# Attention scores of every chunk as float32 products, instead of float32r parts in half of them

## The chip, the cores and the metric

The kernel runs on one core of a Trainium2 chip. The metric is the device time of one launch in microseconds (us), the median of three runs.

## The reference

The program is an attention layer followed by two feed-forward blocks, on two batches of 768 positions. Cut to what matters:

```python
scores = q @ k.T / sqrt(64) + bias          # 8 heads of 64, bias falls with the distance
scores = where(is_global | is_local, scores, -1e9)   # 8 global keys, 96 keys back
a = softmax(scores);  x = a @ v             # (2, 768, 512)
h = relu(x @ w_in)                          # 512 -> 1024
y = (h * sigmoid(conv3(h))) @ w_out         # 1024 -> 512, three taps along the sequence
h = relu(y @ w_in2);  u, v = halves of h
out = (u * (w_spatial @ layernorm(v) + b)) @ w_out2
```

All inputs are float32. q and k enter only in the scores.

## The kernel before

The sequence of each batch is cut into 3 chunks of 256 positions, which gives 6 groups (`g` from 0 to 5). In a group there are 4 units (`u`, a pair of heads each), and in a unit 2 steps (`s`, 128 queries each): 48 steps in all. For one step the following is queued, by the helpers named:

- `qk_load` brings q and k of a unit in one transfer of 336 KB into a tile `qk` (3 buffers). For groups that are not in `NATS` it also makes two parts of it: `qh`, the tile rounded to float32r (cast on ACT), and the rest `qk - qh`, again as float32r, written over `qk` (a subtraction on POOL or DVE, L492 through the helper `parts`).
- `scores` makes the products of both heads of the step on PE (L852). For a group in `NATS` it is one float32 product of `qk` with itself for each head, which the trace shows as two MATMUL records. For the others it is three float32r products for each head: part by part, without the product of the two rests.
- `soften` adds the bias and takes the largest score (L871, DVE), and from group 2 on adds a constant to it (`nb`, L884, POOL or DVE); then the exponential on ACT (L889). `halves` splits the result into float16 parts (`ph`), and a DMA transposes them. `weigh` multiplies with v (L957 for groups 0 and 1, L963 to L965 for the others) and divides by the sum on DVE (L969 to L974, result `xk`). `turn_x` transposes `xk` on PE (L1005) and makes the float16 parts of x.

Beside this run the two feed-forward stages of the first block: `inner` (L1081, 12 products for each of 8 slices of a group; the three taps on DVE, L1094; tanh on ACT; the gate on DVE, L1119) and `outer` (L1151). Their weights come as 64-bit floats and are decoded on ACT (L667) and DVE (L674, L677, L682, tile `wk`): 8 blocks each of the first block's two weights, then 4 blocks of `w3v` and 4 of `w3u` for the second block. After that PE alone carries the second block (L1226, L1299, L1331, L1361).

The order on each engine is written by a planner (`Plan`, lines 97 to 328). It takes every piece of work with a cost that is written beside it, simulates the engines for several rounds, chooses for pieces that two engines can do (POOL or DVE for a subtraction, ACT or DVE for a cast) the one that is done first in its model, and emits the instructions in that order; each engine then works strictly in order. It also puts throwaway matmuls (`warm`, L1052) where its model sees PE idle in the first 70 us. So a changed cost or a missing piece changes the order of the rest too. The cost that `scores` states for a step is 0.79 for float32 and 0.57 for the three float32r products:

```python
        if u // NPAIR in NATS:
            pairs = [(self.m("qk", u), self.m("qk", u))]
            cost, reads = 0.79, [("qk", u)]
        else:
            hi, lo = self.m("qh", u, dt=F32R), self.m("qk", u, dt=F32R)
            pairs = [(hi, hi), (lo, hi), (hi, lo)]
            cost, reads = 0.57, [("qk", u), ("qh", u)]
```

A second way through the program (`dense`) follows for counts beyond the reach of the banded way. It is behind a branch, does not run with these inputs, and the change leaves it alone.

Of the kernel before, what the change touches and what calls it, by code (L numbers as in the profile page):

```python
# [40 lines left out]

LEAD_TICKS, LEAD_STEPS = 12, 8

NATS, PLAINS = (0, 1, 2), (0, 1)

BIASES = 2

# [1589 lines left out]
```

## Time and profile before

| | us |
|---|---|
| runs | 386.78, 386.24, 386.82; median 386.78 |
| the profiled execution | 385.59 |
| its span, first to last instruction | 383.7 |
| outside the span | 1.9 |
| PE busy | 358.4 (93%) |
| DVE busy | 277.9 (72%) |
| ACT busy | 268.4 (70%) |
| POOL busy | 154.7 (40%) |

The durations below are of the one profiled execution, which lies 1.2 us under the median of the runs. All windows and times of the trace are counted from the start of the span. PE is TensorE, DVE VectorE, ACT ScalarE, POOL GpSimd.

### The profile page before, as it was taken

The page shows a single profiled execution, that of the slowest core. Times are in us where ns is not written, and L with a number is a line of the kernel's source. Part 1 is how long each engine was busy: PE and PEld are TensorE (multiplying, and loading weights), DVE is VectorE, ACT ScalarE, POOL GpSimd, SP SyncE. Part 2 cuts the span into 40 slices and gives each one's busy share as a digit, 9 for nine tenths or more (in the row PEclk, how much of TensorE's full clock was granted, in tenths as well). Part 3 has the DMA queues.
Part 4 walks back from the last instruction along what each step waited for, and adds up shares of the span by engine and source line. Part 5 has one row for each costly group of instructions (what it writes and reads, how often), then busy time and mean ns, then how long its engine had stood idle before and what let it go on. Part 6 is the DMA issues. An engine that isn't in the chain of part 4 may idle for free.

```text
span 383.7 us, 7835 instructions
## 1 busy us (share of the span) xinstructions
PE 358.4 (93%) x2852; PEld 252.6 (66%) x2852; DVE 277.9 (72%) x715; ACT 268.4 (70%) x659; POOL 154.7 (40%) x225
## 2 busy tenths in 40 slices
PE   8998788789899999989899999999999999999992
PEld 5777575557778888868689766765456665555541
DVE  5799999998997899999996399881667354241501
ACT  4989797788967999898795499789947434242420
POOL 5254426895778587569653054030205100000000
PEclk9999999899999999999899999999999999999998
DMA  7979523293849557883657000450200000102021
GB/s 221 407 238 296 186 68 91 49 217 109 186 99 240 150 135 128 223 200 57 97 116 297 2 2 0 126 164 2 94 1 2 0 2 15 68 3 81 2 109 64
DMA packets 46254, 43.60 MB, mean 114 GB/s; under 512 B 34816, under 2 KB 36608, under 8 KB 45696
## 3 DMA queue, kind: packets, MB, share of 16 engines
q1 hardware_dynamic: 46208, 43.03, 40.7%
q8 instruction: 24, 0.39, 0.4%
q14 instruction: 22, 0.18, 0.1%
HBM read 31.48 MB, written 3.15 MB: 90 GB/s over the span
## 4 chain that ended last, share of the span: by engine, by line
PE 61%; DVE 21%; ACT 6%; issue 5%; DMA 3%; POOL 2%; SPq 0%; DVEq 0%; POOLq 0%
PE bank L1331 12%; PE bank L1151 10%; PE bank L1081 9%; PE bank L1299 8%; PE bank L1361 8%; PE bank L1226 8%; DVE bank L1094 4%; DVE wk_dt_float L677 3%; DVE sb_dt_float L871 3%; DVE wk_dt_float L682 2%; PE bank L852 2%; DVE wk_dt_float L674 2%; DVE ac_dt_float L1119 2%; ACT sb_dt_float L889 1%; DMA raw_dt_float<-in_w3v 1%
## 5 line engine op out<-in xcount | busy, mean ns | idle before, releaser
L1081 PE MATMUL bank<-x_dt_float,w1h_dt_float 128*128 128x260 f16 (+1 forms) x384 | 65.5, 273 | 5.7 <-DVE xk_dt_float L974 2.5
L1151 PE MATMUL bank<-hh_dt_float,w2l_dt_float 128*128 128x254 f16 (+2 forms) x192 | 53.6, 279 | 1.1 <-POOL w2l_dt_float L492 1.1
L1151 PE MATMUL bank<-hh_dt_float,w2h_dt_float 128*128 128x254 f16 (+2 forms) x192 | 53.8, 280 | 0.2 <-DVE ac_dt_float L1119 0.2
L1151 PE MATMUL bank<-hl_dt_float,w2h_dt_float 128*128 128x254 f16 (+2 forms) x192 | 53.5, 279 | 0.0
L1081 PE MATMUL bank<-x_dt_float,w1l_dt_float 128*128 128x260 f16 (+1 forms) x192 | 52.4, 273 | 0.0
L1094 DVE SCALAR_TENSOR_TENSOR bank<-hp_dt_float,cwt,bank 128x254 f32<-128x254 f32 (+2 forms) x96 | 46.2, 486 | 6.4 <-ACT bank L1088 3.6
L1331 PE MATMUL bank<-ws_dt_float,vn_dt_float 128*128 128x384 f16 x288 | 47.3, 326 | 0.0
L1081 PEld LDWEIGHTS <-w1h_dt_float 128*128 128x128 f16 x384 | 36.6, 97 | 13.2 <-issue 7.6
L492 POOL TENSOR_TENSOR hl_dt_float<-ac_dt_float,hh_dt_float 128x254 f16<-128x254 f32 (+2 forms) x47 | 33.8, 727 | 24.3 <-ACT hh_dt_float L478 21.0
L492 POOL TENSOR_TENSOR ph_dt_float<-sb_dt_float,ph_dt_float 128x512 f16<-128x512 f32 x30 | 38.4, 1283 | 11.6 <-ACT ph_dt_float L478 8.5
L1151 PEld LDWEIGHTS <-w2h_dt_float 128*128 128x128 f16 x384 | 37.0, 100 | 7.3 <-issue 0.7
L1331 PEld LDWEIGHTS <-vn_dt_float 128*128 128x128 f16 x288 | 28.2, 98 | 18.8
L871 DVE CUSTOM_DVE_ANT_0 sb_dt_float<-bank,bias_dt_float 128x256 f32<-128x256 f32 (+1 forms) x96 | 35.0, 401 | 4.7 <-POOL qk_dt_float32r L492 1.7
L889 ACT ACTIVATE sb_dt_float<-sb_dt_float,nb_dt_float 128x256 f32<-128x256 f32 (+1 forms) x64 | 29.6, 493 | 10.5 <-POOL nb_dt_float L884 9.1
L478 ACT CAST g_dt_float<-bank 128x384 f16<-128x384 f32 x16 | 7.7, 479 | 33.8 <-DVE bank L1338 33.8
L1299 PE MATMUL bank<-ys_dt_float,w3uh_dt_float 128*128 128x384 f16 x128 | 31.2, 326 | 0.0
L1335 DVE SCALAR_TENSOR_TENSOR bank<-bank,bb_dt_float 128x384 f32<-128x384 f32 x16 | 9.1, 567 | 29.1 <-PE bank L1331 29.1
L1361 PE MATMUL bank<-w4h_dt_float,g_dt_float 128*128 128x512 f16 (+1 forms) x104 | 28.8, 363 | 0.0
L1226 PE MATMUL bank<-w3vh_dt_float,ys_dt_float 128*128 128x512 f16 x96 | 28.6, 379 | 0.0
L1361 PEld LDWEIGHTS <-g_dt_float 128*128 128x128 f16 x156 | 15.2, 98 | 15.8
L677 DVE SCALAR_TENSOR_TENSOR wk_dt_float<-raw_dt_float,wk_dt_float 128x512 int32<-128x512 int32 x28 | 24.9, 898 | 0.1
L1226 PEld LDWEIGHTS <-ys_dt_float 128*128 128x128 f16 x144 | 14.1, 98 | 15.6
(172 smaller groups left out, 894.0 us busy)
## 6 DMA issues: line engine op xcount, KB each, us to landing
raw_dt_float<-in_w SPq DMA_DIRECT2D x20, 512.0 KB, 5.4
qk_dt_float<-in_qk SPq DMA_DIRECT2D x24, 336.0 KB, 3.9
v_dt_float<-in_vb SPq DMA_DIRECT2D x4, 1024.0 KB, 5.7
out_x<-wk_dt_float SPq DMA_DIRECT2D x11, 256.0 KB, 2.0
raw_dt_float<-in_wst SPq DMA_DIRECT2D x6, 384.0 KB, 4.4
raw_dt_float<-in_w3v SPq DMA_DIRECT2D x4, 512.0 KB, 5.2
raw_dt_float<-in_w3u SPq DMA_DIRECT2D x4, 512.0 KB, 6.3
v_dt_float<-in_vb SPq DMA_DIRECT2D x2, 768.0 KB, 5.9
```

The costliest lines, as they stand in the source:

```text
L492: self.engines[e].tensor_tensor(out=out, in0=in0, in1=in1, op=ALU.subtract)
L677: nc.vector.scalar_tensor_tensor(out=fi, in0=lo, scalar=29, in1=fi, op0=ALU.logical_shift_right, op1=ALU.bitwise_or)
L871: nc.vector.tensor_tensor_reduce(out=sb[:, h, :n], in0=self.ps(self.sp[s][h])[:, :n], in1=self.m("bias", 2 * p + h)[:, t0 : t0 + n], scale ...
L889: nc.scalar.activation(out=sb[:, h, :n], in_=sb[:, h, :n], func=AF.Exp, scale=-1.0, bias=nb[:, h : h + 1])
L1081: nc.tensor.matmul(self.ps(acc)[:, :nx], w[f][:, k * P : (k + 1) * P], x[:, k, x0:], start=k == n == 0, stop=k == 3 and n == 2,)
L1094: nc.vector.scalar_tensor_tensor(out=ac(), in0=near(j), scalar=tap(j), in1=ac(), op0=ALU.mult, op1=ALU.add)
L1151: nc.tensor.matmul(ps(), w[2 * d + k // 4][:, k % 4 * P : (k % 4 + 1) * P], x, start=k == n == 0, stop=k == 7 and n == 2,)
L1226: nc.tensor.matmul(ps(), x[:, y, k, tk], w[k], start=n == 0, stop=n == 11)
L1299: nc.tensor.matmul(ps(), w[e4][:, k * P : (k + 1) * P], x[:, y, k, s], start=n == 0, stop=n == 11)
L1331: nc.tensor.matmul(ps(), v[:, k, x, ek], w[:, k, s], start=n == 0, stop=n == 17)
L1335: nc.vector.scalar_tensor_tensor(out=ps(), in0=ps(), scalar=2.0 ** -(self.k["v"] + self.k["s"]), in1=bb, op0=ALU.mult, op1=ALU.add)
L1361: nc.tensor.matmul(ps(), x[:, y, k, tk], w[k][:, at], start=n == 0, stop=n == 11)
```

## The change

Groups 3, 4 and 5 join groups 0, 1 and 2 in `NATS`. Their 12 units are then not split: 12 casts to `qh` and 12 subtractions go, and the 24 steps of these groups make two float32 products instead of six float32r products. The planner gets neither the split nor the lower cost for these steps and writes a new order for everything.

```diff
-NATS, PLAINS = (0, 1, 2), (0, 1)
+NATS, PLAINS = (0, 1, 2, 3, 4, 5), (0, 1)
```

What the planner makes of it is shown at two places, both on DVE. The first is at the start of group 3's `inner` slices (the tiles `hp` and `ac` belong to them), some 160 us into the program. Before, a decode of `w3v` (L674, L677, tile `wk`) lies between the taps, ahead of the division that gives `xk`:

```order
L1094 SCALAR_TENSOR_TENSOR bank<-hp_dt_float_180,cwt,bank 128x254 x2
L1119 SCALAR_TENSOR_TENSOR ac_dt_float_177<-bank,hp_dt_float_176 128x254
L674 TENSOR_SCALAR wk_dt_float_125<-wk_dt_float_125 128x512
L1119 SCALAR_TENSOR_TENSOR ac_dt_float_181<-bank,hp_dt_float_180 128x254
L677 SCALAR_TENSOR_TENSOR wk_dt_float_125<-raw_dt_float_140,wk_dt_float_125 128x512
L1094 SCALAR_TENSOR_TENSOR bank<-hp_dt_float_184,cwt,bank 128x254 x2
L969 TENSOR_SCALAR r_dt_float_158<-bank,cs_dt_float_215 128x4
L973 RECIPROCAL r_dt_float_158<-r_dt_float_158 128x4
L974 TENSOR_TENSOR xk_dt_float_150<-bank,r_dt_float_158 128x256
```

After the change, from the row behind the first one above, the same stretch of DVE reads:

```order
L1119 SCALAR_TENSOR_TENSOR ac_dt_float_177<-bank,hp_dt_float_176 128x254
L492 TENSOR_TENSOR x_dt_float_154<-bank,x_dt_float_153 128x256
L1119 SCALAR_TENSOR_TENSOR ac_dt_float_181<-bank,hp_dt_float_180 128x254
L1094 SCALAR_TENSOR_TENSOR bank<-hp_dt_float_184,cwt,bank 128x254 x2
L871 ISA sb_dt_float_137,nm_dt_float_151<-bank,bias_dt_float_307 128x256
L871 ISA nm_dt_float_151 128x1
L871 ISA sb_dt_float_137,nm_dt_float_151<-bank,bias_dt_float_313 128x256
L871 ISA nm_dt_float_151 128x1
L1119 SCALAR_TENSOR_TENSOR ac_dt_float_185<-bank,hp_dt_float_184 128x254
L969 TENSOR_SCALAR r_dt_float_158<-bank,cs_dt_float_210 128x4
L973 RECIPROCAL r_dt_float_158<-r_dt_float_158 128x4
L974 TENSOR_TENSOR xk_dt_float_150<-bank,r_dt_float_158 128x256
```

The decode of the `w3v` blocks has left the stretch; it follows when the slices of this group are done.

The second place is late in the lead, where the last blocks of `w2` are decoded while group 1's attention runs, some 66 us into the program. The rows marked - are of before, those marked + of the change:

```order
 L682 SCALAR_TENSOR_TENSOR wk_dt_float_125<-raw_dt_float_124,wk_dt_float_125 128x512
+L674 TENSOR_SCALAR wk_dt_float_127<-wk_dt_float_127 128x512
+L674 TENSOR_SCALAR wk_dt_float_134<-wk_dt_float_134 128x512
+L677 SCALAR_TENSOR_TENSOR wk_dt_float_127<-raw_dt_float_126,wk_dt_float_127 128x512
+L677 SCALAR_TENSOR_TENSOR wk_dt_float_134<-raw_dt_float_133,wk_dt_float_134 128x512
 L969 TENSOR_SCALAR r_dt_float_158<-bank 128x4
 L973 RECIPROCAL r_dt_float_158<-r_dt_float_158 128x4
 L974 TENSOR_TENSOR xk_dt_float_150<-bank,r_dt_float_158 128x256
-L674 TENSOR_SCALAR wk_dt_float_127<-wk_dt_float_127 128x512
-L674 TENSOR_SCALAR wk_dt_float_134<-wk_dt_float_134 128x512
```

Here four instructions of the decode moved ahead of the division that PE's L1005 waits for.

## Rows read from the trace of the kernel before

**Rows 1.** The page: its span, and the chain that ended last by engine.

```profile
span 383.7 us, 7835 instructions
...
PE 61%; DVE 21%; ACT 6%; issue 5%; DMA 3%; POOL 2%; SPq 0%; DVEq 0%; POOLq 0%
```

**Rows 2.** Windows: length, busy us of PE, PEld, DVE, ACT, POOL, then PE's granted clock, DMA.

```profile
70.00:75.00 5.00, 4.87 (x27) 3.34 (x28) 5.00 (x12) 3.17 (x10) 3.54 (x4) 0.66 0.12 13
...
110.00:155.00 45.00, 45.00 (x478) 36.28 (x476) 39.40 (x122) 39.45 (x92) 31.84 (x50) 1.00 0.70 160
155.00:185.00 30.00, 26.86 (x311) 22.23 (x308) 28.35 (x80) 25.45 (x67) 22.18 (x31) 1.00 0.66 152
180.00:185.00 5.00, 3.66 (x51) 3.06 (x49) 4.93 (x13) 2.61 (x6) 3.62 (x6) 1.00 0.32 61
185.00:190.00 5.00, 4.53 (x26) 3.37 (x26) 5.00 (x10) 3.78 (x11) 4.70 (x4) 0.66 0.39 74
...
200.00:375.00 175.00, 175.00 (x1116) 107.23 (x1114) 94.68 (x179) 99.21 (x241) 27.96 (x36) 1.00 0.16 55
```

**Rows 3.** Waits of PE from 76 to 204 us: total, times, longest.

```profile
PE bank L1005 <- DVE xk_dt_float L974: 2.7, 3, 1.8
PE bank L1081 <- DVE xk_dt_float L974: 1.2, 1, 1.2
PE bank L963 <- DVE ac_dt_float L1119: 1.2, 2, 0.8
PE bank L776 <- DVE vm_dt_float L757: 1.0, 1, 1.0
```

**Rows 4.** The same view from 0 to 76 us.

```profile
PE bank L1005 <- DVE xk_dt_float L974: 3.1, 2, 2.4
```

**Rows 5.** PE's timeline, a float32 and a float32r step: start, duration, instruction.

```profile
79.42 0.70 PE L852 MATMUL bank<-qk_dt_float 64*128 64x256 f32 x4
80.06 0.28 PE L1151 MATMUL bank<-hh_dt_float,w2h_dt_float 128*128 128x254 f16 x1
...
87.62 0.39 PE L852 MATMUL bank<-qh_dt_float32r 64*128 64x256 f32 x2
...
88.17 0.28 PE L1151 MATMUL bank<-hh_dt_float,w2h_dt_float 128*128 128x254 f16 x1
```

**Rows 6.** Lines by form: the split of q and k, and a DVE subtraction.

```profile
L492 POOL TENSOR_TENSOR qk_dt_float32r<-qk_dt_float,qh_dt_float32r 128x672 fp32r<-128x672 f32 x10 | 16.6, 1661 | 3.8 <-ACT qh_dt_float32r L478 2.0 <-DMA qk_dt_float<-in_qk 1.6
...
L478 ACT CAST qh_dt_float32r<-qk_dt_float 128x672 fp32r<-128x672 f32 x12 | 8.9, 744 | 0.8 <-DMA qk_dt_float<-in_qk 0.8
...
L492 DVE TENSOR_TENSOR qk_dt_float32r<-qk_dt_float,qh_dt_float32r 128x672 fp32r<-128x672 f32 x2 | 2.7, 1328 | 0.0
L492 DVE TENSOR_TENSOR ph_dt_float<-sb_dt_float,ph_dt_float 128x512 f16<-128x512 f32 x2 | 2.6, 1303 | 0.0
```

**Rows 7.** DVE's timeline at group 3's slices: the `w3v` decode among them.

```profile
161.87 1.17 DVE L674 TENSOR_SCALAR wk_dt_float<-wk_dt_float 128x512 int32<-128x512 int32 x1
...
163.29 1.06 DVE L677 SCALAR_TENSOR_TENSOR wk_dt_float<-raw_dt_float,wk_dt_float 128x512 int32<-128x512 int32 x1
```

**Rows 8.** DVE's timeline before the stop at 183.7 us.

```profile
179.64 1.11 DVE L884 TENSOR_TENSOR nb_dt_float<-nm_dt_float,shift 128x2 f32<-128x2 f32 x1
...
182.57 0.41 DVE L488 SCALAR_TENSOR_TENSOR ys_dt_float<-bank,ys_dt_float 128x258 f16<-128x258 f32 x1
...
184.20 0.42 DVE L674 TENSOR_SCALAR wk_dt_float<-wk_dt_float 128x512 int32<-128x512 int32 x1
```

**Rows 9.** DVE's timeline behind the division at 68.1 us.

```profile
68.43 1.93 DVE L674 TENSOR_SCALAR wk_dt_float<-wk_dt_float 128x512 int32<-128x512 int32 x2
70.28 1.64 DVE L677 SCALAR_TENSOR_TENSOR wk_dt_float<-raw_dt_float,wk_dt_float 128x512 int32<-128x512 int32 x1
...
72.53 0.95 DVE L677 SCALAR_TENSOR_TENSOR wk_dt_float<-raw_dt_float,wk_dt_float 128x512 int32<-128x512 int32 x1
```

**Rows 10.** DVE's timeline early: the wait before the first division.

```profile
14.15 0.16 DVE L969 TENSOR_SCALAR r_dt_float<-bank 128x4 f32<-128x4 f32 x1 [1.61 <-PE bank L957]
```

## The prediction

> **What bounds the kernel now.** I read the page's span and chain first, then windows by stage, then PE's waits, then the timelines at the waits. The chain names PE for 61% and DVE for 21% of the span [rows 1], so the question is where which of the two leads. The windows answer it: from 110 to 155 us PE is busy for all of its 45 us, and from 200 to 375 us for all of its 175 us [rows 2]. There only PE's own work counts, and nothing that DVE, ACT or POOL are spared brings anything. From 155 to 185 us it is the other way: PE is busy for 26.9 of 30 us, DVE for 28.4 [rows 2]. The waits say for what PE stands still there: the longest are 1.8 us and 1.2 us for `xk`, the division on DVE [rows 3]. The lead, up to 85 us, is of the same kind, with a wait of 2.4 us for `xk` as its longest [rows 4]. Twice the granted clock of TensorE falls from 2.4 to 1.2 GHz: in the windows 70 to 75 and 185 to 190 us its mean is 0.66 [rows 2], which is 3.4 us at half speed and so about 1.7 us of work lost each time. Both falls come after PE stood still: after the wait of 2.4 us, and after 180 to 185 us, where PE is busy for 3.7 of 5 us [rows 2, 4].
>
> So the program's time is PE's work, plus PE's waits before 200 us, plus the two slow stretches, plus the end. The change touches the first three.
>
> **The change part by part.**
>
> *The products themselves (PE, slower).* A float32 step with float16 neighbours goes from 79.42 to 80.06 us until the next matmul starts, 0.64 us; a float32r step from 87.62 to 88.17 us, 0.55 us [rows 5]. The other steps repeat this pattern to 0.01 us. The difference, 0.09 us less rounding, is 0.08 us. With 24 steps that is +2.0 us, on the engine that sets the end. This price needs no bound, since both forms are in the trace. By the Trainium skill, "FP8 and Floating Point Precision", section "TensorE Precision Notes", a true float32 product takes four passes through the array. Read with one pass for each float32r product that makes four in place of three, +0.18 us for a step, 4.4 us in all and a sum that is 2.4 us worse; the rows speak against it here, since the four records of the float32 step take 15% longer than the six of the other, not 33%.
>
> *The split (ACT, POOL, DVE: removed).* 12 casts of 0.74 us on ACT, 10 subtractions of 1.66 us on POOL, 2 of 1.33 us on DVE [rows 6]: 8.9, 16.6 and 2.7 us of busy time. ACT and POOL end no long wait of PE after 76 us [rows 3], so what they are spared counts at zero by itself, covered by DVE's queue; if DVE were not the late one, POOL would be. The 2.7 us on DVE are real only where DVE leads, and the planner gives part of them away: it now puts one subtraction of a `w2` block on DVE in the lead, and one of `ph` there too. The nearest row is the `ph` subtraction, of the same size, 1.30 us [rows 6]: +2.6 us against one split subtraction of 1.3 us gone from that stretch. Against that it moves the first decode into a wait of 1.6 us which DVE has at 14 us [rows 10], of which I count all. The lead then comes to 2.6 - 1.3 - 1.6 = -0.3 us. The ends are +1.3 us (nothing of that wait is used) and -1.6 us (the added subtractions find room); I take **-0.5 us**, the middle less a little for POOL's emptier queue.
>
> *The decode of `w3v` among group 3's slices (DVE, moved).* Two decode instructions of 1.17 and 1.06 us stand between the taps just before the division that PE waits 1.2 us for [rows 3, 7]. In the new order they follow after the slices. So this wait should go. They are not gone from DVE, though: they still run before the next long wait, the one of 1.8 us at 183.7 us. Ahead of that one three others leave: the addition of `nb` (1.11 us, now on POOL), an instruction of `ys` (0.41 us) and one L674 (0.42 us), both put behind the division [rows 8]. Start to start, less 0.08 us of overlap each for the last two, that is 1.8 us which DVE is early. PE however comes earlier too: by the 1.2 us of the wait that went, less 5 steps of 0.08 us that lie between the two places, so by 0.8 us. The wait at 183.7 us then is 1.8 - 1.8 + 0.8 = 0.8 us. Both together fall from 3.0 us to 0.8 us, **-2.2 us**. Bounds: 0, if the first wait only moves to the second place; -3.0 us, if both go.
>
> *The slow stretch at 185 us.* With a wait of 0.8 us in place of 1.8 us, and none some us before, I expect the clock to stay at 2.4 GHz: **-1.7 us**. Bounds: 0 and -1.7.
>
> *Waits added.* None by the change itself: the scores now wait for the load of `qk` alone, where they waited for a cast and a subtraction behind it. The throwaway matmuls go from 42 to 38; they lie in PE's idle time, so they count at zero unless the clock falls in their place.
>
> *Sum.* +2.0 - 0.5 - 2.2 - 1.7 = -2.4 us. The profiled execution took 385.6 us (383.7 us of span and 1.9 us around it), which gives 383.2 us; it lies 1.2 us under the median of the runs, so against the median of 386.8 us the forecast is **384.4 us**.
>
> **The rivals.** What a measurement can tell from no change is about 0.2%, 0.8 us; that is the border between the cases.
>
> *The clock falls all the same at 185 us.* PE is busy for only 3.7 of 5 us there [rows 2], and part of that idle time may be spread over small waits. Then the sum is -0.7 us: 386.1 us, just inside the border.
>
> *The waits only move (slower).* DVE is busy for 28.4 of the 30 us from 155 us [rows 2]. If the decode, now in one lump after the slices, holds up the division at 183.7 us by what the earlier place gained, neither wait nor slow stretch goes: +2.0 - 0.5 = +1.5 us, 388.3 us. It decides from the point at which that wait is 3 us or more. For it: the lump stands on DVE right ahead of that place; against it: three instructions left the same queue [rows 8].
>
> *The lead stops longer (slower).* At the wait of 2.4 us in the lead [rows 4] four decode instructions now stand ahead of the division instead of behind it. Behind it they take 1.93, 1.64 and 0.95 us [rows 9], 4.3 us start to start. If the wait grows by that, if it isn't given back by a shorter queue afterwards, and if the slow stretch that follows lasts twice as long (1.7 us), the sum is +2.0 + 4.3 + 1.7 - 2.2 - 1.7 = +4.1 us: 390.9 us. For it: DVE is busy for all of the 5 us from 70 us [rows 2], so it is what counts there. Against it: the same work is no longer behind the division, so DVE should be early for what comes next; the lead's end is then the same.
>
> *A larger relief.* POOL's queue shrinks by a tenth, and DVE's L674 takes 1.17 us in one place and 0.42 us in another [rows 7, 8], on the same shape. If the longer times come from POOL's subtractions running beside it, less POOL work shortens DVE's too. Then both waits go (-3.0), and those of 1.2 and 1.0 us from 85 us on [rows 3] with them: +2.0 - 0.5 - 3.0 - 1.7 - 2.2 = -5.4 us, 381.4 us. Taking the lead at its bound of -1.6 us it is 380.3 us. By the Trainium skill, "SBUF — State Buffer", section "Who interferes with whom", DVE and GpSimd share one pair of ports, which one of them holds for a whole instruction, so that the other blocks. The two durations agree with it; the sum with it is this rival's, and it has no share in the forecast's.
>
> *Four passes,* as weighed above: 386.8 us, no change.
>
> *The split isn't gone.* It is: in the new order no float32r instruction is left in the part that runs.
>
> **How the numbers follow.** The forecast 0.46; the clock falls all the same 0.15; the waits only move 0.11; the lead stops longer 0.11; the larger relief 0.13; four passes 0.04. Faster by over 0.2% are the forecast, the larger relief and somewhat under half of the clock's case: 0.65. Within 0.2% are the rest of that case, four passes, and a small part of the waits that only move: 0.15. Slower is what is left: 0.20. The likeliest case alone, with its bounds for the lead and for the second wait, goes from 382.6 to 386.2 us. The range for 8 in 10 leaves out the lead that stops longer and the last part of the larger relief, and takes in the waits that only move: 380.8 to 388.4 us.
>
> **What would show it.** Right: L852 has 192 float32 records, and a step takes 0.64 us; no L492 and L478 with float32r tiles; PE's wait for `xk` around 164 us is gone and the one near 183 us under 1 us; the granted clock is at 2.4 GHz from 180 to 200 us; from 110 us to about 155 us and from 200 us PE is still busy without a gap. Wrong: a second slow stretch that stays, PE's waits after 150 us still 3 us in sum, or waits in the lead, 0 to 76 us, that grow by more than 2 us. If steps took 0.74 us, the price of the products would be the failed step.

## The result, and the profile after

The kernel after takes **383.26 us** (median of 5 runs, 382.01 to 384.14), the kernel before 386.78 us: a ratio of 0.991, with a 95% interval from 0.9885 to 0.9935. That is 3.5 us, or 0.9%, faster. The profiled execution took 382.87 us and has a span of 381.0 us, against 385.59 and 383.7 us.

First the page of the kernel after: the span, the busy time of each engine, the chain by engine.

```profile
span 381.0 us, 7688 instructions
...
PE 358.0 (94%) x2800; PEld 248.5 (65%) x2800; DVE 270.4 (71%) x710; ACT 260.5 (68%) x646; POOL 137.2 (36%) x219
...
PE 59%; DVE 15%; ACT 10%; POOL 7%; issue 6%; DMA 2%; POOLq 0%; DVEq 0%; ACTq 0%
```

PE is busy for as long as before (358.0 and 358.4 us), although its products became dearer; one slow stretch of its clock fewer (below) is part of the reason. DVE lost 7.5 us of busy time, ACT 7.9 and POOL 17.5. In the chain DVE fell from 21 to 15% [rows 1], ACT rose from 6 to 10% and POOL from 2 to 7%.

The step is the first term of the prediction. The timeline of PE (start, duration, instruction), a float32 step of group 3 and what follows it:

```profile
114.80 0.70 PE L852 MATMUL bank<-qk_dt_float 64*128 64x256 f32 x4
115.43 0.44 PE L1005 MATMUL bank<-ident,xk_dt_float 128*128 128x128 f32 x2
```

From one start to the next it is 0.63 us. The 24 steps of groups 3 to 5 now all look like this, where the float32r form took 0.55 us [rows 5].

The windows of the kernel after, with the columns of [rows 2]:

```profile
70.00:75.00 5.00, 4.65 (x41) 3.80 (x38) 5.00 (x14) 3.38 (x10) 3.50 (x4) 1.00 0.96 101
110.00:155.00 45.00, 44.25 (x457) 34.02 (x455) 37.62 (x118) 35.73 (x85) 22.68 (x44) 1.00 0.64 148
155.00:185.00 30.00, 29.27 (x295) 22.76 (x293) 27.43 (x74) 26.50 (x71) 20.86 (x31) 1.00 0.64 160
180.00:185.00 5.00, 4.32 (x33) 3.12 (x32) 4.97 (x7) 2.75 (x7) 5.00 (x5) 1.00 0.56 107
185.00:190.00 5.00, 4.22 (x51) 3.30 (x51) 4.19 (x17) 2.49 (x6) 3.47 (x4) 1.00 0.56 105
200.00:375.00 175.00, 173.32 (x1091) 105.07 (x1087) 94.00 (x179) 95.62 (x232) 30.54 (x37) 1.00 0.16 55
```

From 155 to 185 us PE is busy for 2.4 us more than before. Both windows with a clock of 0.66 are now at 1.00, which is 2.4 GHz. One slow stretch, 3.4 us at half speed, stands early, where the kernel before had none:

```profile
25.00:30.00 5.00, 4.38 (x22) 2.75 (x22) 4.86 (x18) 4.30 (x12) 2.46 (x3) 0.71 0.60 161
```

PE's waits from 76 to 204 us, which answer to [rows 3], in total, times, longest:

```profile
PE bank L1005 <- DVE xk_dt_float L974: 1.3, 2, 0.6
PE bank L963 <- DVE ac_dt_float L1119: 1.3, 2, 0.8
PE bank L852 <- DVE nm_dt_float L871: 0.8, 1, 0.8
```

and from 0 to 76 us [rows 4]:

```profile
PE bank L1005 <- DVE xk_dt_float L974: 3.4, 2, 2.8
PE bank L1081 <- DVE nm_dt_float L871: 2.1, 1, 2.1
```

The wait of 1.2 us for `xk` in front of L1081 is gone, and the one of 1.8 us. In their place stand shorter ones, and a new one of 2.1 us in the lead.

The two kernels can be set against each other at one place in any order of the rest: the transpose of the last division (L1005), after which PE works alone. Of before, and below it of after:

```profile
206.57 0.38 PE L1005 MATMUL bank<-ident,xk_dt_float 128*128 128x128 f32 x2
```

```profile
203.71 0.38 PE L1005 MATMUL bank<-ident,xk_dt_float 128*128 128x128 f32 x2
```

It comes 2.86 us earlier. Behind it 177.1 and 177.3 us are left, the same. So in these two executions, whose spans differ by 2.7 us, the whole gain arose before 206 us. The question of the experiments is by which of the change's three parts: dearer products, no split, another order.

### The profile page after: what moved, and what is told of

Read it like the earlier page. It is cut to its first block, busy times and chain, and to the rows that moved or that the text cites. A ratio compares the mean times of both kernels' runs of the same rounds, so it can differ in the third digit from the quotient of the medians.

```text
span 381.0 us, 7688 instructions
## 1 busy us (share of the span) xinstructions
PE 358.0 (94%) x2800; PEld 248.5 (65%) x2800; DVE 270.4 (71%) x710; ACT 260.5 (68%) x646; POOL 137.2 (36%) x219
## 4 chain that ended last, share of the span: by engine, by line
PE 59%; DVE 15%; ACT 10%; POOL 7%; issue 6%; DMA 2%; POOLq 0%; DVEq 0%; ACTq 0%
PE bank L1331 12%; PE bank L1151 8%; PE bank L1299 8%; PE bank L1361 8%; PE bank L1226 8%; PE bank L1081 6%; PE bank L852 3%; DVE bank L1094 3%; DVE sb_dt_float L871 3%; ACT sb_dt_float L889 3%; DVE wk_dt_float L677 2%; POOL ph_dt_float L492 2%; DVE wk_dt_float L682 2%; POOL hl_dt_float L492 2%; ACT ph_dt_float L478 2%
## 5 line engine op out<-in xcount | busy, mean ns | idle before, releaser
L1081 PE MATMUL bank<-x_dt_float,w1h_dt_float 128*128 128x260 f16 (+1 forms) x384 | 65.3, 273 | 3.0 <-DVE nm_dt_float L871 2.1
L1151 PE MATMUL bank<-hh_dt_float,w2h_dt_float 128*128 128x254 f16 (+2 forms) x192 | 52.4, 273 | 1.0 <-DVE nm_dt_float L871 1.0
L1151 PE MATMUL bank<-hl_dt_float,w2h_dt_float 128*128 128x254 f16 (+2 forms) x192 | 52.3, 272 | 0.5 <-POOL hp_dt_float L1103 0.4
L1081 PE MATMUL bank<-x_dt_float,w1l_dt_float 128*128 128x260 f16 (+1 forms) x192 | 52.3, 273 | 0.0
L1151 PE MATMUL bank<-hh_dt_float,w2l_dt_float 128*128 128x254 f16 (+2 forms) x192 | 52.3, 272 | 0.0
L492 POOL TENSOR_TENSOR ph_dt_float<-sb_dt_float,ph_dt_float 128x512 f16<-128x512 f32 x30 | 37.3, 1249 | 22.7 <-ACT ph_dt_float L478 19.3
L1081 PEld LDWEIGHTS <-w1h_dt_float 128*128 128x128 f16 x384 | 36.7, 97 | 9.9 <-issue 4.6
L889 ACT ACTIVATE sb_dt_float<-sb_dt_float,nb_dt_float 128x256 f32<-128x256 f32 (+1 forms) x64 | 29.5, 492 | 15.3 <-POOL nb_dt_float L884 14.5
L852 PE MATMUL bank<-qk_dt_float 64*128 64x256 f32 x192 | 34.6, 441 | 0.8 <-DVE nm_dt_float L871 0.8
L677 DVE SCALAR_TENSOR_TENSOR wk_dt_float<-raw_dt_float,wk_dt_float 128x512 int32<-128x512 int32 x28 | 27.4, 982 | 0.2
```

The lines of the kernel that those rows point to most:

```text
L492: self.engines[e].tensor_tensor(out=out, in0=in0, in1=in1, op=ALU.subtract)
L677: nc.vector.scalar_tensor_tensor(out=fi, in0=lo, scalar=29, in1=fi, op0=ALU.logical_shift_right, op1=ALU.bitwise_or)
L852: nc.tensor.matmul(self.ps(sp[h])[:, :256], x[r, t * P : (t + 1) * P], y[r, k0 : k0 + 256], start=n == 0, stop=n == len(pairs) - 1,)
L889: nc.scalar.activation(out=sb[:, h, :n], in_=sb[:, h, :n], func=AF.Exp, scale=-1.0, bias=nb[:, h : h + 1])
L1081: nc.tensor.matmul(self.ps(acc)[:, :nx], w[f][:, k * P : (k + 1) * P], x[:, k, x0:], start=k == n == 0, stop=k == 3 and n == 2,)
L1151: nc.tensor.matmul(ps(), w[2 * d + k // 4][:, k % 4 * P : (k % 4 + 1) * P], x, start=k == n == 0, stop=k == 7 and n == 2,)
```

## The experiments

Theories at the start. **A**, the prediction's: the products cost 2.0 us, the split is worth little by itself, the new order takes PE's waits away. **B**: the removed work itself is the gain. **C**: only slow stretches of the clock count. Each experiment was run 6 to 12 times beside runs of the kernel before on the same chip (median there 386.35, 386.66 and 387.00 us in the three groups of four). The ratios and their 95% intervals are to those; they go by the single runs and so differ by up to 0.4% from the quotients of the medians. A difference between two experiments is taken from their ratios; from the intervals I estimate that it is uncertain by about 0.3%, 1.2 us.

**The three parts, one at a time.** The planner is left in the belief that the work is as before, so the order stays that of before, word for word; only the emitted instructions change.

The first kernel has the products of after and no split:

```diff
-            pairs = [(hi, hi), (lo, hi), (hi, lo)]
+            pairs = [(self.m("qk", u), self.m("qk", u))]
...
-        self.parts(
-            CH + KW, self.m("qh", u, dt=F32R), self.m("qk", u, dt=F32R), self.m("qk", u),
-            [("qk", u)], [("qh", u)], [("qk", u)],
-        )
+        self.plan.add(copy_cost(CH + KW), lambda e: None, reads=[("qk", u)], writes=[("qh", u)])
+        self.plan.add(sub_cost(CH + KW), lambda e: None, reads=[("qk", u), ("qh", u)], writes=[("qk", u)])
```

> The order of before, with the 24 steps of groups 3 to 5 as float32 products and no instruction for the split (12 casts on ACT, 10 subtractions on POOL, 2 on DVE are gone; the planner still thinks they are there, so nothing else moves). Theory A (mine: the products cost +2.0 us, the split is worth little by itself, the new order takes PE's waits for xk away): +2.0 us, less up to 1.3 us for the DVE subtraction in the lead: 387.5 to 388.8 us against 386.8, PE's waits for xk at about 164 and 184 us still there, in sum 2 us or more. Theory B (the removed work itself is the gain: POOL's and DVE's relief shortens what PE waits for): 384 to 385.5 us in the old order too, with both waits gone. Theory C (only the granted clock counts, one slow stretch fewer): 388.8 us with a slow stretch near 70 and near 186 us, about 387 us with one of them gone, and no other difference.

Measured: 384.97 us, ratio 0.9951 (0.9928 to 0.9974), so 1.9 us faster than before. A, which expected it slower, falls. It is the time that B gave, but not B's way there: in this trace the first of PE's two waits for `xk` is as long as before, 1.24 us, and only the other shrank, from 1.81 to 1.13 us. And it is short of the kernel after.

The second makes the split, writes its rest over `qh` in place of `qk`, and reads neither:

```diff
-            CH + KW, self.m("qh", u, dt=F32R), self.m("qk", u, dt=F32R), self.m("qk", u),
+            CH + KW, self.m("qh", u, dt=F32R), self.m("qh", u, dt=F32R), self.m("qk", u),
```

> As the run before, but the 12 casts and 12 subtractions run as in the kernel before; what they write (the rounded copy, with the rest written over it) is read by nothing, and the products read q and k as loaded. This is the price of the products by itself. Theory A: 24 x 0.08 = +2.0 us, 388.8 us, within 0.5 us of it; the difference to the run without the split is what the removed work is worth, 0 to 1.3 us. Theory B: 388.8 us as well, but 3 us or more above the run without the split. Theory C: as A, where the slow stretches stay where they were.

Measured: 387.21 us, ratio 1.0011 (0.9988 to 1.0034). The products by themselves cost +0.4 us, with 2.0 us outside the interval (-0.5 to +1.3). The step itself has the price that the prediction gave it, so a part of it is covered, about half by the two profiled executions: PE is 1.60 us later than before at 162 us, 1.25 us later behind the two waits for `xk`, and 1.09 us at 207 us. (The products here no longer wait for the split either. That brought nothing where it could be seen: the one long wait of DVE that named POOL's split subtraction before, 1.67 us at 118.6 us, is 1.81 us here and names PE.) And the split that nobody reads is worth 0.6% of the time, 2.3 us, in an order that doesn't change.

The first kernel was run again, since its profiled execution had been its longest of 12:

> The kernel of the first experiment once more, unchanged, since its profiled execution was the longest of its 12 and its granted clock low for 6.8 us near 25 us and 13.6 us near 69 us. The worth of the split rests on it: 385.0 us again within 0.5 us, and in a profile with short slow stretches the tail behind the last division is 177.1 us and the last division comes at about 206 us, 1.7 us earlier than with the idle split.

Measured: 384.80 us, ratio 0.9943 (0.9918 to 0.9968), 2.6 us under the idle split. C falls as well: this execution has a slow stretch near 70 us and none at 186, for which C gave about 387 us, and took 385.01; and the mean clock of the 12 runs is 0.983, of the kernel before beside them 0.982. This trace has the order of before, so it can be laid over it row by row. PE's timeline from 182 us, of before:

```profile
185.47 0.44 PE L1005 MATMUL bank<-ident,xk_dt_float 128*128 128x128 f32 x2 [1.81 <-DVE xk_dt_float L974]
190.10 0.39 PE L852 MATMUL bank<-qh_dt_float32r 64*128 64x256 f32 x2
...
194.07 0.38 PE L1005 MATMUL bank<-ident,xk_dt_float 128*128 128x128 f32 x2
200.34 0.38 PE L1005 MATMUL bank<-ident,xk_dt_float 128*128 128x128 f32 x2
```

and of the old order without the split (the line that was shown, 206.57 us, is at 205.91 here), with the earlier wait of 1.2 us [rows 3] as its first row:

```profile
166.12 0.38 PE L1081 MATMUL bank<-x_dt_float,w1h_dt_float 128*128 128x256 f16 x2 [0.39 <-DVE xk_dt_float L974]
...
184.98 0.44 PE L1005 MATMUL bank<-ident,xk_dt_float 128*128 128x128 f32 x2 [1.12 <-DVE xk_dt_float L974]
187.95 0.70 PE L852 MATMUL bank<-qk_dt_float 64*128 64x256 f32 x4
192.31 0.44 PE L1005 MATMUL bank<-ident,xk_dt_float 128*128 128x128 f32 x2 [0.15 <-DVE xk_dt_float L974]
198.88 0.44 PE L1005 MATMUL bank<-ident,xk_dt_float 128*128 128x128 f32 x2
205.91 0.38 PE L1005 MATMUL bank<-ident,xk_dt_float 128*128 128x128 f32 x2
```

The slow stretch at 186 us is gone here too, in the old order. Follow the lead over before from 184.98 us on: 0.49 us there, 2.15 at the next row, then 1.76, 1.46 and 0.66 at the last. The full clock brings 1.7 us within 3 us of time, and 1.5 us of it is given back within the next 18, where waits for DVE and POOL appear that the slow PE had not had. DVE's own pace shows why: from the division that ends the second long wait to the last division it takes 20.02 us before, with the slow stretch, and 20.02 and 20.01 us in the idle split and here, without. **This slow stretch, in which PE was not the late engine, cost next to nothing.** Nor did a shorter wait prevent it: in the idle split's trace the wait ahead of it is still 1.60 us long, and the clock stays at 2.4 GHz.

In the lead it looks alike. In this trace the clock is low for 10 us from 71 us on:

```profile
70.00:75.00 5.00, 4.49 (x23) 3.30 (x23) 5.00 (x10) 2.83 (x10) 3.91 (x4) 0.63 0.16 21
75.00:80.00 5.00, 5.00 (x25) 4.05 (x25) 4.48 (x12) 4.12 (x9) 4.44 (x4) 0.50 1.10 194
80.00:85.00 5.00, 5.00 (x35) 3.06 (x34) 2.62 (x12) 2.71 (x9) 3.44 (x7) 0.85 0.88 262
```

and a transpose that stands at 78.41 us in before comes at 81.67, but one at 100.16 us comes at 100.44:

```profile
81.67 0.44 PE L1005 MATMUL bank<-ident,xk_dt_float 128*128 128x128 f32 x2
100.44 0.38 PE L1005 MATMUL bank<-ident,xk_dt_float 128*128 128x128 f32 x2
```

3.3 us behind, and 20 us later 0.3. But the split is missing between the two as well, and slow stretches are not free in general. The first run of this same kernel has 13.6 us at half speed there, and 6.8 us more near 25 us: it is 1.13 us later than this one at 75 us, still 1.13 us at 162 us, and 2.4 us from 168 us to the end, as its wait near 166 us is longer too. And of the 29 runs of the kernel before in the first group the nine with a mean clock up to 0.977 took 387.3 us in the median, the 13 with 0.986 or more 386.0 us. Their mean clocks differ by 0.016, which is 6.0 us of PE's work, and their times by 1.3 us: by this estimate some fifth of what a slower clock takes away reaches the end.

Against the idle split the trace of the second run is 1.75 us ahead at 207 us: 0.26 us of that at 111 us, 0.99 us at the wait near 166 us and 0.49 us at the one near 185 us. The next experiments show what acts at these two.

**What of the split counts.** First the two of its subtractions that stood on DVE, then the ten on POOL, are left out of the idle split, each by the engine that the planner chose:

```diff
-        self.parts(
...
+        qh, qk, drop = self.m("qh", u, dt=F32R), self.m("qk", u), ("DVE",)
+        self.plan.add(
+            copy_cost(CH + KW), lambda e: e in drop or self.copy(e, qh, qk), reads=[("qk", u)], writes=[("qh", u)],
+        )
+        self.plan.add(
+            sub_cost(CH + KW), lambda e: e in drop or self.minus(e, qh, qk, qh), reads=[("qk", u), ("qh", u)],
+            writes=[("qk", u)],
+        )
```

New theories: **D**, DVE's queue leads, and what DVE is spared counts; **E**, POOL's subtractions lengthen DVE's instructions beside them.

> The order of before, float32 products, the split run and read by nothing, but without the two of its subtractions that stood on DVE (2.7 us of busy time); the 12 casts on ACT and the 10 subtractions on POOL run. With the split whole the time was 387.2 us, without any of it 385.0. Theory D (new: before 206 us the queue of DVE leads and PE's extra 2.0 us are mostly covered, so what counts is what DVE is spared): 385 to 385.7 us. Theory E (what counts is POOL: its subtractions lengthen DVE's instructions that run beside them): 387.2 us within 0.6 us. Theory A: 386 to 387 us, the subtraction of the lead alone.

Measured: 386.93 us, ratio 1.0013 (0.9988 to 1.0038), as with the split whole. D falls in this form: 2.7 us less on the engine with the latest queue bring nothing that can be measured.

> The complement: the order of before, float32 products, the 12 casts on ACT and the two subtractions on DVE run and are read by nothing; the 10 subtractions on POOL (16.6 us) are gone. Theory D: 386.5 to 387.5 us, as with the split whole. Theory E: 385 to 385.7 us, as without it, and DVE's mean time of one instruction L674 or L677 lower than in the run with the split whole.

Measured: 386.45 us, ratio 0.9988 (0.9967 to 1.0009), 0.9 us under the idle split: a part, not the whole of E's 2 us, and less than the uncertainty. E's second sign is there in L674 (564 ns against 844 in the idle split, from 76 to 207 us), not in L677 (973 against 975).

Then the casts alone and all the subtractions alone. Theory **D2** is that the parts add up, **E2** that the subtractions hurt only together.

```diff
+        self.plan.add(copy_cost(CH + KW), lambda e: None, reads=[("qk", u)], writes=[("qh", u)])
+        self.plan.add(sub_cost(CH + KW), lambda e: self.minus(e, qh, qk, qk), reads=[("qk", u), ("qh", u)], writes=[("qk", u)])
```

> The order of before, float32 products, the 12 casts on ACT left out; the 12 subtractions run (qk less qk, read by nothing). Whole idle split 387.2 us, without DVE's share 386.9, without POOL's 386.5, without any 385.0: if the parts add up, the casts are worth the remaining 1.3 us, and this run gives 385.9 us, within 0.5 us (theory D2: ACT's queue ends waits too). If the subtractions only hurt together (POOL's and DVE's both in the way, theory E2), 387 us.

Measured: 385.36 us, ratio 0.9967 (0.9947 to 0.9988). Without the 12 casts on ACT the time falls by 1.7 us, though the subtractions all run. They no longer wait for a cast, as POOL's did in the idle split for 2.2 us, so this is not ACT's time alone.

```diff
+        self.plan.add(copy_cost(CH + KW), lambda e: self.copy(e, qh, qk), reads=[("qk", u)], writes=[("qh", u)])
+        self.plan.add(sub_cost(CH + KW), lambda e: None, reads=[("qk", u), ("qh", u)], writes=[("qk", u)])
```

> The order of before, float32 products, all 12 subtractions left out, the 12 casts run and are read by nothing. Theory D2: the casts' 1.3 us remain, 386.3 us. Theory E2: as without any split, 385.0 us within 0.5 us.

Measured: 386.05 us, ratio 0.9977 (0.9957 to 0.9998), 1.3 us under the idle split. Casts 1.7 and subtractions 1.3 make 3.0 where 2.3 and 2.6 were measured for both. Each of these ratios is uncertain by 0.2%, so this says that they roughly add up, and not which part is the larger.

How the split acts can be read at PE's two long waits for `xk`, in the eight traces that have the old order (all in us; "way" is DVE's time from the division before to the one that PE waits for):

| runs of the split | ACT near 158 us waits for the weights of `w3v` | ACT waits there for `nb` | PE's wait near 166 us | DVE's way to the second wait | PE's wait near 185 us |
|---|---|---|---|---|---|
| all, with float32r products (before) | 1.26 | 0 | 1.23 | 12.22 | 1.81 |
| all (idle split) | 0.26 | 0.70 | 1.24 | 12.22 | 1.60 |
| without DVE's | 0.27 | 0.69 | 1.24 | 12.21 | 1.60 |
| subtractions only | 0.09 | 0.56 | 1.07 | 12.06 | 1.44 |
| without POOL's | 1.36 | 0 | 1.23 | 11.74 | 1.13 |
| casts only | 0.12 | 0 | 0.42 | 11.75 | 1.13 |
| none, first run | 1.36 | 0 | 1.24 | 11.73 | 1.13 |
| none, second run | 0.05 | 0 | 0.39 | 11.73 | 1.12 |

At the first wait it is ACT that holds up DVE's taps, and with them the division behind them. In the idle split POOL's subtraction stands in front of the addition L884, for which the exponential on ACT waits (POOL's timeline, then ACT's):

```profile
158.05 2.06 POOL L492 TENSOR_TENSOR qh_dt_float32r<-qk_dt_float,qh_dt_float32r 128x672 fp32r<-128x672 f32 x1
160.06 0.20 POOL L884 TENSOR_TENSOR nb_dt_float<-nm_dt_float,shift 128x2 f32<-128x2 f32 x1
```

```profile
160.30 0.51 ACT L889 ACTIVATE sb_dt_float<-sb_dt_float,nb_dt_float 128x256 f32<-128x256 f32 x1 [0.70 <-POOL nb_dt_float L884]
```

Without POOL's subtractions this goes. But ACT's part of the `w3v` decode, L667, stands there too and waits for its weights to land, as in before:

```profile
157.81 0.68 ACT L667 ACTIVATE wk_dt_float<-raw_dt_float 128x512 f32<-128x512 f32 x1 [1.26 <-DMA raw_dt_float<-in_w3v]
```

With and without the split this happens in some traces: the two of the one kernel without the split have 1.36 and 0.05 us of it. PE's wait is short only where neither holds ACT up.

At the second wait theory E holds: without POOL's split subtractions DVE's way is 0.5 us shorter, in all four traces. From 76 to 207 us the decode L674 on DVE (busy us, mean ns) before, and with the subtractions but no casts:

```profile
L674 DVE TENSOR_SCALAR wk_dt_float<-wk_dt_float 128x512 int32<-128x512 int32 x5 | 3.8, 760 | 0.0
```

```profile
L674 DVE TENSOR_SCALAR wk_dt_float<-wk_dt_float 128x512 int32<-128x512 int32 x5 | 2.8, 563 | 0.0
```

The two means differ by one instruction on that way. Before, a subtraction of `ph` ran on POOL beside it (DVE's timeline, then POOL's):

```profile
181.27 1.38 DVE L674 TENSOR_SCALAR wk_dt_float<-wk_dt_float 128x512 int32<-128x512 int32 x1
```

```profile
179.13 3.24 POOL L492 TENSOR_TENSOR ph_dt_float<-sb_dt_float,ph_dt_float 128x512 f16<-128x512 f32 x2
```

With the casts gone POOL was through before it began:

```profile
181.88 0.41 DVE L674 TENSOR_SCALAR wk_dt_float<-wk_dt_float 128x512 int32<-128x512 int32 x1
```

```profile
178.17 3.17 POOL L492 TENSOR_TENSOR ph_dt_float<-sb_dt_float,ph_dt_float 128x512 f16<-128x512 f32 x2
```

It is so throughout. In the 14 traces the 156 L674 with no TENSOR_TENSOR on POOL beside them take 0.39 to 0.46 us, the 78 with at least 0.7 us of one beside them 0.69 to 1.41 us. The gate L1119 on DVE, which reads a `bank`, takes 0.39 to 0.43 us with and without. At this place, then, the split lengthens DVE's decode at second hand: it decides when POOL's other subtractions come. In the trace with the subtractions other instructions caught it (L677 1.00 us for 0.87, L682 1.64 for 1.16), and DVE's way is only 0.16 us shorter. Without any split the five of the way that reach such lengths (L674, L677, L884 and twice L682) take 4.52 us together, before 5.18.

**The split put back into the new order.** The kernel after, with every instruction in its place, and 12 casts on ACT and 12 subtractions on POOL added as idle work:

```diff
+            if casts and e == "ACT" and start > self.landed(casts[0][0], when):
+                subs.append((when[i][1] + act(CH + KW), casts[0][2]))
+                casts.pop(0)[1]()
+            elif subs and e == "POOL" and start > subs[0][0]:
+                subs.pop(0)[1]()
```

> The order and the products of the kernel after, with the split put back as idle work: 12 casts on ACT and 12 subtractions on POOL, each behind the first instruction of the plan there for which the data have landed, read by nothing; every other instruction keeps its place. Theory D: DVE's queue is the one of the kernel after, so 383.3 us within 0.8 us. Theory E: +2 us or more, 385.3 us. Theory A: 383.3 us (ACT and POOL end no long wait).

Measured: 397.08 us, ratio 1.0233 (1.0185 to 1.0281, without the longest of the six), and every theory missed it: against the 0.991 of the kernel after that is 3.2%, over 12 us. Its waits from 85 to 180 us, on ACT:

```profile
ACT sb_dt_float L905 <- POOL nb_dt_float L900: 13.1, 5, 3.0
```

The same in the kernel after:

```profile
ACT sb_dt_float L889 <- POOL nb_dt_float L884: 5.2, 5, 1.8
```

and on POOL and ACT at one such place:

```profile
167.64 1.60 POOL L503 TENSOR_TENSOR qh_dt_float32r<-qk_dt_float,qh_dt_float32r 128x672 fp32r<-128x672 f32 x1
169.20 0.35 POOL L900 TENSOR_TENSOR nb_dt_float<-nm_dt_float,shift 128x2 f32<-128x2 f32 x2
```

```profile
169.44 0.91 ACT L905 ACTIVATE sb_dt_float<-sb_dt_float,nb_dt_float 128x256 f32<-128x256 f32 x2 [2.78 <-POOL nb_dt_float L900]
```

A subtraction of 1.6 us stands in front of an addition of two numbers for each position (L900 here, L884 in the kernels without the added code), and ACT's exponential waits for that addition. In the kernel after POOL is busy for 36% of the span and is still on the path: the exponential of each step from group 2 on hangs on it where POOL makes the addition. But this does not account for the 12 us. The window from 85 to 180 us holds less of the work here; up to the last division ACT's wait for the addition is 19.6 us here and 14.5 us in the kernel after. The 12 casts on ACT came too, the profiled execution is that longest one, and the mean clock of the six is 0.968, of the kernel after 0.984 (its second ten runs, below). No run separates these. In the order of before the planner knew of the split: its subtractions stand elsewhere, and two of these additions are on DVE.

**The order alone.** Three kernels differ only in the price that the planner is told for a step. The kernel before, with 0.79 in place of 0.57:

```diff
-            cost, reads = 0.57, [("qk", u), ("qh", u)]
+            cost, reads = 0.79, [("qk", u), ("qh", u)]
```

> The kernel before with its float32r products and its split; only the price that the planner takes for a float32r step is raised from 0.57 to 0.79 us, so that it writes another order for the same work. Theory A: the order alone moves the time, by more than 0.8 us in either direction (384.5 to 388.5 us), because it sets PE's waits before 200 us. Theory B: the work is the same, so 386.8 us within 0.8 us. Theory C: the time differs by 1.7 us for each slow stretch more or fewer, and by nothing else.

Measured: 391.07 us, ratio 1.0118 (1.0086 to 1.015): 4.6 us for the same work in another order, and outside the 384.5 to 388.5 us of A and the 386.0 to 387.6 us of B. Of the 5.3 us between the two profiled executions 2.0 us stand before the last division (208.61 us) and 3.3 us behind it. The kernel after with 0.64, the measured price, in place of 0.79:

```diff
-            cost, reads = 0.79, [("qk", u)]
+            cost, reads = 0.64, [("qk", u)]
```

> The kernel after, where the planner takes 0.64 us for a float32 step, as measured, in place of 0.79 us (groups 0 to 5). The work is that of the kernel after, the order another. Theory A: PE's time is the same and the waits before 200 us differ: 381.5 to 385.5 us against 383.3. Theory B: 383.3 us within 0.8 us, since the same work is gone. Theory C: 383.3 us, less or more 1.7 us for each slow stretch fewer or more.

Measured: 387.97 us, ratio 1.0026 (1.0002 to 1.0049). The whole gain is gone, with the true price; A, which gave at most 385.5 us, and B miss it. And with 0.57 there:

> A third order for the work of the kernel after: the planner takes 0.57 us for a float32 step (groups 0 to 5) in place of 0.79 us. With 0.64 us the time was 388.0, with 0.79 us 383.3. If an order's time is a matter of which waits it happens to leave (theories A and D), it lies anywhere between 382 and 389 us, and its difference to 383.3 us is the sum of PE's waits before 206 us and not the tail behind the last division, which stays at 177.1 us. If the price itself decides (a higher price leaves PE room), it is above 388.0 us.

Measured: 391.01 us, ratio 1.01 (1.007 to 1.0131). Three orders of one work lie at 383.3, 388.0 and 391.0 us, and the last lies outside the 382 to 389 us of theories A and D. For the kernel after a higher price gave the faster order each time, for the kernel before it gave the slower one, so the price is no rule. The tail was 174.8 us here, not 177.1: the last division comes at 214.3 us, and some of what PE does behind it in the other orders has been done before. In the order with 0.64 us the clock is low three times in the lead, some 17 us in all:

```profile
25.00:33.00 8.00, 6.84 (x32) 4.22 (x32) 7.86 (x27) 6.35 (x20) 2.45 (x2) 0.57 0.93 279
46.00:54.00 8.00, 8.00 (x40) 6.13 (x40) 6.47 (x19) 5.42 (x15) 4.22 (x7) 0.57 0.54 172
80.00:84.00 4.00, 4.00 (x18) 2.51 (x20) 4.00 (x13) 2.46 (x8) 2.48 (x5) 0.57 0.65 146
```

How much of its 4.7 us over the kernel after comes from that, and how much from its waits, no run here separates.

Last, the kernel after once more, beside the second run of the old order without the split:

> The kernel after once more on the same chip as the old order without the split, so that the two can be set against each other: the work is the same, the order another. If the new order is worth anything, it is faster by 0.8 us or more: 383.3 us against 385.0. If not, both agree within 0.8 us and the whole gain is the removed split.

Measured: 382.97 us, ratio 0.991 (0.9878 to 0.9942), against 0.9943 for the same work in the old order. The new order is worth 0.3 to 0.4%, 1.3 to 1.6 us. The intervals overlap at their ends, and the second pair alone would not be clear of the noise, but both pairs of runs say the same: 383.26 and 384.97, 382.97 and 384.80 us. No run was faster than the kernel after, so there is no better version to show.

## Why the prediction was right or wrong

The forecast was 384.4 us, 1.1 us above the time, which lies inside the range, and the sign was right. Of its four terms the first was right as a price only, the second stays open, the third came about but in part by another cause, and the fourth came about and was worth next to nothing. What the runs put in their stead is +0.4 for the products (idle split against before), -2.3 or -2.6 for the removed split (no split against idle split, two runs) and -1.6 or -1.3 for the order (the kernel after against no split). The three are steps from one kernel to the next, so they add up to the measured -3.5 us by themselves.

*The products, +2.0 us.* The price of a step was right (0.63 us against 0.55). The failed part is "with 24 steps that is +2.0 us, on the engine that sets the end". The runs with the idle split show +0.4 us (-0.5 to +1.3). From 110 to 163 us PE does fall behind by 0.08 us with every step, as predicted, and has collected 1.0 us there; but two long waits for DVE and a stretch led by DVE and POOL still lie ahead, and an engine that arrives later at a wait waits less. Not all of it goes there, since DVE itself waits for PE's products: in the profiled executions 1.60 us at 162 us have become 1.09 us at 207 us. A window in which PE is busy for all of 45 us [rows 2] told only that PE led there, not that what it loses there reaches the end.

*The split, counted at zero by itself.* This is the step that failed most: "ACT and POOL end no long wait of PE after 76 us, so what they are spared counts at zero". PE's waits name the last link alone. DVE, which they name, waits for ACT, and ACT's exponential for POOL's addition: 0.70 us of this stand behind the first wait for `xk` in the idle split and are gone without POOL's subtractions. And POOL's work lengthens DVE's: without the split on POOL, DVE's way to the second wait is 0.5 us shorter. Where the rest of the gain comes from, the casts' share above all, is not shown. Taking away 8.9 us on ACT and 16.6 us on POOL brought 2.3 to 2.6 us with no reorder at all, while the 2.7 us on DVE, half of which was the only share that was given a value, brought nothing measurable.

*The lead, -0.5 us.* The first L776 comes at 83.11 us, before at 85.45 us, but the orders differ so much there that the two don't mark the same state of the work, and the slow stretch moved from 70 to 27 us. The size of this term stays open. The lead's own waits did not grow by more than 2 us in sum: the one for `xk` went from 2.4 to 2.8, a new one of 2.1 came, and others went; PE is busy for 65.96 us of the first 76, before 65.19. From 110 to 155 us, where no gap was expected, PE lost 0.75 us to one wait for the gate on DVE (L963 above).

*The waits for `xk`, -2.2 us.* The wait near 164 us went, as said, and the one near 183 us fell under 1 us. But the reasons were others in part. For the first, the prediction blamed two decode instructions on DVE. Before, ACT's instruction of the same decode, L667, waits 1.26 us for its weights ahead of them; and in the old order the wait is down to 0.4 us in the two traces where nothing holds ACT up, with both DVE instructions still in place. In the new order L667 has left the stretch together with them, so that the step came true and its reason was incomplete. The second wait falls from 1.8 to 1.1 us in the old order as soon as POOL's split subtractions are gone; only the rest can belong to the new order, and no run shows by which instruction.

*The slow stretch, -1.7 us.* It went, and PE kept 2.4 GHz from 180 to 200 us as the forecast said. Its worth was wrong: 1.7 us gained and 1.5 given back by 206 us, where it was taken away in the old order. So was its reason, a shorter wait ahead of it: with the idle split it goes although that wait is 1.60 us. The term was sized as if PE led from the stretch on. It does so from about 206 us; between 190 and 206 us PE of the kernel before had no gap only because the stretch had made it late.

*The rivals.* That the clock falls all the same, that the waits only move, that the lead stops longer, that the products take four passes: none came. The larger relief, given 0.13, was right in its mechanism and too large in its size: the L674 of 1.17 us stands beside a subtraction of `ph` on POOL, that of 0.42 us does not. By the Trainium skill, "SBUF — State Buffer", section "Who interferes with whom", DVE and GpSimd share a pair of ports. The traces agree with it for L674: 0.39 to 0.46 us with no TENSOR_TENSOR on POOL beside it, up to 1.41 us beside one. At the second wait this is worth 0.5 us; the other waits that this case has going, those of 1.2 and 1.0 us from 85 us on, became 1.3 us (L963) and 0.7 us (L776).

The terms that were too high and those that were too low cancelled, which was luck. The number was closer than the reasons.

## What to carry to other kernels

Work that is removed from engines that are often idle can still be worth more than what it costs the busy one: follow the wait one link further, from the engine that PE waits for to the one which that engine waits for. Before charging a loss on the leading engine, or a slow stretch of its clock, look at what lies between it and the end: a wait for another engine takes the loss out again as far as that engine isn't made late by it too, here nearly all of the slow stretch at 186 us and about half of the dearer products. Before calling a wait gone, look at a second trace of the same kernel: one wait was 1.24 us in one and 0.39 us in the other. And where a planner writes the order, measure the same work in two or three orders first: here three orders lie up to 7.7 us apart, twice the effect that was to be judged.

## What the runs showed of the hardware that was not expected

The two true float32 products of a step, one for each head, take 15% longer than the six float32r products, 0.63 us against 0.55, and save the whole split besides.

DVE's L674, which reads and writes int32 and has no `bank` among its operands, takes 0.39 to 0.46 us with no TENSOR_TENSOR on POOL beside it and up to 1.41 us beside one; the gate L1119, which reads a `bank`, takes 0.39 to 0.43 us either way.

The granted clock varies from run to run of one kernel, and the time follows it only loosely: the kernel before took 386.35 us in a run with a mean of 0.997 and 385.31 us in one with 0.982, while over its 29 runs in the first group a mean clock lower by 0.016 goes with a time longer by 1.3 us, where 6.0 us of PE's work are lost (the estimate above). Where the loss falls decides: at 186 us, with PE ahead of DVE, 3.4 us at half speed (1.2 GHz) cost nothing that could be seen at DVE's divisions.
